# The hand-over between two mixture-of-experts layers: last token tile in two column halves, one joined sending of two tiles, two weight pieces split earlier, loads and PSUM banks in another order

## The chip, the cores and the metric

One core of one Trainium2 chip runs the whole program in one launch. The metric is the device time of that launch in microseconds (us); lower is better. Three runs of the kernel before give 742.63, 743.99 and 744.5 us, with a median of 743.99.

## What is computed

Three layers follow each other on N = 1536 tokens (2 batches of 768) of width 512. Everything is float32.

```
x   = attention with per-head decay (8 heads of 64, blocks of 64)      # [1536, 512]
x   = sum over 4 experts e of p[:, e] * (relu(x @ w1[e]) @ w2[e])      # dense: every token, hidden width 1024
l   = x @ w_gate; expert = argmax(l); gate = softmax(l)[expert]        # 8 experts, one per token
out = gate * (relu(x @ w1b[expert]) @ w2b[expert])                     # sparse: only the chosen expert
```

The change lies where the second line ends and the fourth begins.

## The kernel before

**Tiles and precision.** A token tile is 128 tokens; there are `NC` = 12. `acc[:, t, 0:512]` holds the rows of token tile t in SBUF, column `DM` = 512 its gate weight, column 513 its token number. For precision a float32 operand is split in a high and a low part: ScalarE casts the high part (`A.copy`, L195), VectorE subtracts it for the low part (L197). A matrix product is then three products: high with high, low with high, high with low (`mm3`, L572). Weights come from HBM in pieces of 512 KB (`load_piece`, L145) into tiles `raw`, each of which holds two column blocks; `split_to` (L289) does the next splits of a fixed list, and each piece whose second block is split frees its `raw` tile and issues the next load (`drop_raw`, L168). There are four such tiles, and two more (`raw2`) from the sparse layer on.

**Order of the work.** Every engine executes its own queue in program order; the order is written by hand (`tc.manual_schedule`), and a place in it is where a function is called. SP's queue issues the loads, and a load whose tile isn't free, or whose rows aren't written, holds back all that stand behind it.

**End of the dense layer** (loop at L1260 to L1287). For the last two tiles, y = 10 and z = 11, TensorE computes the hidden tiles `ht` and then for each token tile the product `y` (24 matmuls of 512 columns, `moe1_mm2`, L608), which VectorE scales and adds into `acc` (L623).

**Routing of a token tile.** `route_x` (L819) transposes `acc` on TensorE and copies it to SBUF. `route_choose` (L827) multiplies it with the gate weights (`lg`, L835) and finds the largest logit on VectorE (`mx`, `sc`, `m2`, `oh`, `df`, `seen`). `route_place` (L869) counts with two small matmuls (`rank`) how many tokens before it chose the same expert, and VectorE makes from it the row `pos` of the DRAM table `bins` to which the token goes. `route_row` (L896) writes the gate weight into `acc`, and GpSimd scatters the 128 rows into `bins` (L121).

**First expert without the round trip.** The sparse layer begins with expert 0, at most 176 tokens. Its rows of the first ten tiles are read back from `bins` (`first_load`, tile `xe`) and transposed into PSUM (`first_T`, tiles `px`, four of them, one for each 128 columns). The rows of tiles y and z never leave the chip: `first_sel` (L938) builds a 0/1 matrix `sel` from `pos`, and `first_place` (L945) adds `acc` times `sel` to `px` (8 matmuls a tile). `rows_split` (L1315) splits the four `px` into `xg`, the input of expert 0. Idle spots of TensorE are filled with products of ones (`keep_up`, L1012).

**Sparse layer** (L1531 on). `route_order` (L954) sorts the other seven experts by their token counts, on VectorE, and leaves their numbers in `nth`. SP reads these with a register load (`values_load`), loads the rows of an expert from `bins` (`load_rows`, L1331, tile `xb`) and the weights of experts 1 to 7, whose addresses depend on `nth` too. For an expert e, TensorE makes eight products `g` (L1374, L1375), VectorE and ScalarE turn them into hidden tiles and, between these, split the second weights `w1h`, `w1l` (`hook1`); then follow four products `z`, and behind each of them (`hook2`) the transposes `xt` of the next expert's rows `xb` (`rows_T`, L1347) and splits of the next first weights. In the profile the first `z` of expert 0 needs all eight hidden tiles. For experts with 129 to 255 tokens (`WIDE`) a product takes two columns blocks at once, and ScalarE (L1377) and VectorE (L1378) add the two halves in a tile of the tag `yt`.

Of the kernel before, what the change touches and what calls it, by code (L numbers as in the profile page):

```python
# [67 lines left out]
FAR = 1 << 20  # L68
OMAX = (N - min(CAPS[0], BY_RANK[0]) + P - 1) // P
# [4 lines left out]
def body(ctx: ExitStack, tc: tile.TileContext, lam, att, dp, w1a, w2a, wg, wgt, w1b, w2b, out):  # L74
# [91 lines left out]
    st = {}  # L166

# [11 lines left out]
    def split_plain(n, c, only=""):  # L179
# [7 lines left out]
        hi, lo = wt[b]  # L187
        t = raw_q[0][:, c % 2]
        if b[0] == 0 and k < K1 and half(k) == 0:
            hi, lo = (x[:, :, c * P:c * P + P] for x in (hi, lo))  # L190
            t = t.rearrange("p (d f) -> p d f", d=KD)
        else:
            hi, lo = hi[:, c, :], lo[:, c, :]
# [434 lines left out]

    def open_fast():
# [124 lines left out]
    def open_routing():  # L754
# [13 lines left out]
        rp = rt["rs"] = rt_ctx.enter_context(pool("rs", 2, side="right"))  # L768
# [50 lines left out]
    def route_x(t):  # L819
        tr = rt["ps_rt"].tile([P, KD, P], F32, tag="rtr", name=f"rtr{t}")  # L820
        for d in range(KD):
            T.transpose(tr[:, d, :], acc[:, t, d * P:d * P + P], ident)
        xt = rt["rp"].tile([P, KD, P], F32, tag="xt", name=f"xt{t}")
        A.copy(out=xt, in_=tr)
        rt[t, "xt"] = xt

    def route_choose(t, midway=None):  # L827
        rp = rt["rs"]
        if t < VT:
            lg = lg_v[:, t, :]  # L830
        else:
            xt = rt.pop((t, "xt"))
            lg = small(f"lg{t}")[:, :E2]
            for d in range(KD):
                T.matmul(lg, xt[:, d, :], wg_sb[:, d, :], start=d == 0, stop=d == KD - 1)  # L835
# [13 lines left out]
        if midway:  # L849
            midway()  # L850
        V.tensor_scalar(
            out=ec, in0=m2, scalar1=-float(MOST), scalar2=float(E2 * MOST), op0=ALU.mult,
            op1=ALU.add,
        )
# [13 lines left out]

    def route_place(t):  # L869
        rp = rt["rs"]  # L870
        oh, ec, df, prev = rt.pop((t, "chosen"))
# [3 lines left out]
        rank = small(f"rank{t}")[:, :E2]  # L875
        T.matmul(rank, upper, oh, start=True, stop=prev is None)
        if prev is not None:
            T.matmul(rank, ones, prev, start=False, stop=True)
# [26 lines left out]

    def first_load():
# [8 lines left out]
    def first_T(s):  # L915
        if s == 0:
            rt["px"] = [
                ps_mm.tile([P, 512], F32, tag="mm", name=f"px{d}") if d < 3 else
                rt["ps_rt"].tile([P, 512], F32, tag="rtr", name=f"px{d}") for d in range(KD)
            ]  # L920
        for d in range(KD):
            T.matmul(
                rt["px"][d][:, s * ST:s * ST + ST], rt["xe"][:ST, s, d * P:d * P + P],
                ident[:ST, :ST], start=s == 0, stop=False, is_transpose=True,
            )

    def first_high(t):
        ah = rt["fp"].tile([P, DM], F32R, tag="ah", name=f"ah{t}")
        A.copy(out=ah, in_=acc[:, t, 0:DM])
        rt[t, "ah"] = ah  # L930

    def first_low(t):
        ah = rt.pop((t, "ah"))
        al = rt["fp"].tile([P, DM], F32R, tag="al", name=f"al{t}")
        V.tensor_tensor(out=al, in0=acc[:, t, 0:DM], in1=ah.bitcast(F32), op=ALU.subtract)
        rt[t, "parts"] = (ah, al)

    def first_sel(t):  # L938
        sel = rt[t, "sel"] = rt["fp"].tile([P, CAP], F32R, tag="sel", name=f"sel{t}")
        V.tensor_scalar(  # L940
            out=sel, in0=rt["slots"].rearrange("p s i -> p (s i)"), scalar1=rt[t, "pos"],
            scalar2=None, op0=ALU.is_equal,
        )

    def first_place(t):  # L945
        for d in range(KD):
            for i, part in enumerate(rt[t, "parts"]):
                T.matmul(
                    rt["px"][d][:, :CAP], part[:, d * P:d * P + P], rt[t, "sel"], start=False,
                    stop=t == NC - 1 and i == 1,  # L950
# [3 lines left out]
    def route_order():  # L954
        count, place, places = od["count"], od["place"], od["places"]
        by_pair = od["tmp"][:, :EN * EN].rearrange("p (a b) -> p a b", a=EN)
        sm = small("counts")[:, :E2]
# [54 lines left out]
    def keep_up(n):  # L1012
        warmup(small("warm_rt"), n)


    with tc.manual_schedule():
# [240 lines left out]
        st_ctx.close()  # L1257
        open_last()

        for t0 in range(TS, N, 256):  # L1260
# [16 lines left out]
            for j in range(256 // P):  # L1277
                if t0 // P + j == NC - 1:
                    assert not plan
                    first_load()  # L1280
                    first_high(NC - 2)
                    split_to(0, K1 + 1, 2)
                    first_low(NC - 2)
                    moe1_mm2(KL, hs, t0, j, lambda: route_x(NC - 2))
                    continue
                moe1_mm2(KL, hs, t0, j)
                unit(2 * FC + j)  # L1287
# [12 lines left out]
        first_sel(z)  # L1300
        keep_up(4)
        first_place(z)
        route_row(y)
        route_row(z)
# [15 lines left out]
        for d in range(KD):  # L1320
            rows_split(xg[0][0][:, d, :], xg[0][1][:, d, :], rt["px"][d][:, :CAP])
# [9 lines left out]
        def load_rows(e):  # L1331
            if e >= E2:
                return
            if e:
# [4 lines left out]
                )  # L1339
            xb = gp.tile([P, NMOST, W], F32, tag="xb", name=f"xb{e}", bufs=4)  # L1340
# [27 lines left out]
        def product(e, ps, parts):  # L1368
# [7 lines left out]
            s = gp.tile([P, MOST], F32, tag="yt", name=f"s{ps.name}", bufs=4)[:, :n]  # L1376
# [374 lines left out]
```

## Time and profile before

| | before |
|---|---|
| median of 3 runs | 743.99 us |
| lowest and highest | 742.63, 744.5 us |
| profiled execution | 742.62 us |
| its span, first to last instruction | 740.8 us |
| TensorE (PE) busy | 729.9 us, 99% of the span |
| VectorE (DVE) busy | 510.6 us, 69% |
| ScalarE (ACT) busy | 312.2 us, 42% |
| share of the last-ending chain on PE | 95% |
| mean granted clock of TensorE | 0.997 |

The profile is of one execution; times in it count from the first instruction. A row of the timeline gives the start, the duration, the engine, the line of the source, the operation, its output and inputs (without buffer numbers) and how many instructions it merges; in brackets stands the idle time of the engine before it and what ended that. Instructions of one engine overlap a little, so the distance from one start to the next tells what one costs in a row, and the duration when its result is there. PEld is TensorE's loading of weights, which overlaps its matmuls.

### The profile page before, as it was taken

Reading aid. Unit: us, or ns where it says so; the run is one execution under the profiler, and the core shown is the slowest. Engines: PE = TensorE matmul, PEld = TensorE weight load, DVE = VectorE, ACT = ScalarE, POOL = GpSimd, SP = SyncE. Lnnn points to the kernel's source line nnn. Section 1 sums busy time; section 2 is a strip of 40 time slices with the busy share of each in tenths; the row PEclk is TensorE's granted clock in tenths of the full one; section 3 lists DMA queues with packets and bytes.
Section 4 is the critical chain, followed back from the end, with each engine's and each line's share of the span. In section 5 each row is a group of like instructions: output and inputs, shape, how many; then the busy total and the mean of one; then the engine's idle time right before and its main releaser. Section 6 shows DMA issues by size and latency. Waiting matters only on the chain.

```text
span 740.8 us, 12994 instructions
## 1 busy us (share of the span) xinstructions
PE 729.9 (99%) x4956; PEld 660.7 (89%) x4956; DVE 510.6 (69%) x1142; ACT 312.2 (42%) x688; POOL 80.5 (11%) x86
## 2 busy tenths in 40 slices
PE   9999999999999999999999999999999999999995
PEld 8888989889898998989889898998899998998994
DVE  7557867676766766657666667774678867675883
ACT  4333735344352434434223041631134747566672
POOL 3464000000000000000000002100021013121013
PEclk9999999999999999999999999999999999999998
DMA  8862893636446175546161443351143968765661
GB/s 314 302 217 87 282 290 111 256 115 254 162 151 256 71 270 227 176 181 231 48 247 60 196 180 135 97 201 40 52 116 124 322 212 274 249 212 184 235 222 31
DMA packets 39420, 136.79 MB, mean 185 GB/s; under 512 B 6913, under 2 KB 6913, under 8 KB 34747
## 3 DMA queue, kind: packets, MB, share of 16 engines
q1 hardware_dynamic: 37243, 129.63, 50.2%
q0 software_dynamic: 2112, 6.31, 2.2%
q8 instruction: 40, 0.66, 0.4%
q14 instruction: 25, 0.20, 0.1%
HBM read 102.85 MB, written 33.26 MB: 184 GB/s over the span
## 4 chain that ended last, share of the span: by engine, by line
PE 95%; DVE 3%; issue 1%; ACT 0%; POOL 0%; POOLq 0%; ACTq 0%
PE y L582 37%; PE b L706 26%; PE h L582 7%; PE g L582 5%; PE z L582 3%; PE z L1374 2%; PE zr L1482 2%; PE gr L582 2%; PE qk L382 1%; PE z L1375 1%; PE xo L516 1%; DVE w1l L197 1%; PE g L1374 1%; PE zr L1453 1%; PE warm L1010 1%; PE xt L1356 1%
## 5 line engine op out<-in xcount | busy, mean ns | idle before, releaser
L623 DVE SCALAR_TENSOR_TENSOR acc<-y,p_sb,acc 128x512 f32<-128x512 f32 x78 | 58.6, 751 | 67.6 <-PE y L582 60.6
L197 DVE TENSOR_TENSOR w1l<-raw,w1h 128x512 fp32r<-128x512 f32 x128 | 85.0, 687 | 29.2 <-ACT w1h L195 28.7
L713 ACT COPY u<-b 128x384 f32<-128x384 f32 x78 | 36.4, 477 | 110.1 <-PE b L706 109.1
L195 ACT CAST w1h<-raw 128x512 fp32r<-128x512 f32 x128 | 75.4, 617 | 1.7 <-DMA raw<-in_w2a 1.7
L121 POOL DMA_INDIRECT bins<-acc,pos x12 | 13.1, 1092 | 474.7 <-DVE mx L842 380.4
L706 PE MATMUL b<-xh,w0h 128*128 128x384 f32 x208 | 57.8, 338 | 0.0
L197 DVE TENSOR_TENSOR w0l<-raw,w0h 128x512 fp32r<-128x512 f32 x76 | 50.3, 707 | 0.2
L812 DVE CUSTOM_DVE_ANT_0 x<-acc,x 128x512 f32<-128x512 f32 x72 | 49.4, 687 | 1.0
L195 ACT CAST w0h<-raw 128x512 fp32r<-128x512 f32 x76 | 43.0, 622 | 2.7 <-DMA raw<-in_w1a 2.7
L720 DVE TENSOR_TENSOR u<-b,u 128x384 f32<-128x384 f32 x78 | 43.0, 552 | 1.4 <-PE b L706 1.4
L121 POOL DMA_INDIRECT out<-y,xb x16 | 29.2, 1828 | 135.4 <-DVE y L1516 84.9
L706 PEld LDWEIGHTS b<-xh,w0h 128*128 128x128 f32 x208 | 38.2, 188 | 0.6
L582 PE MATMUL g<-xg,w0h 128*128 128x288 f32 (+1 forms) x192 | 38.1, 293 | 0.0
L582 PE MATMUL h<-xh,w0h 128*128 128x256 f32 x144 | 36.0, 292 | 0.3 <-ACT xh L176 0.3
L706 PE MATMUL b<-xl,w0h 128*128 128x384 f32 x104 | 35.3, 339 | 0.0
L582 PE MATMUL h<-xh,w0l 128*128 128x256 f32 x144 | 34.6, 281 | 0.1
L706 PE MATMUL b<-t1h,w0h 128*128 128x384 f32 x104 | 31.0, 339 | 0.0
L582 PEld LDWEIGHTS g<-xg,w0h 128*128 128x128 f32 x192 | 30.9, 189 | 0.0
L1374 PE MATMUL z<-g,w1h 128*128 128x352 f32 (+2 forms) x96 | 29.1, 366 | 0.8 <-DVE g L1396 0.7
L706 PE MATMUL b<-t2h,w0l 128*128 128x384 f32 x104 | 28.9, 339 | 0.0
L706 PE MATMUL b<-t4h,w0l 128*128 128x384 f32 x104 | 28.9, 339 | 0.0
L706 PE MATMUL b<-t3h,w0h 128*128 128x384 f32 x104 | 28.8, 338 | 0.0
(328 smaller groups left out, 2038.9 us busy)
## 6 DMA issues: line engine op xcount, KB each, us to landing
raw<-in_w2a SPq DMA_DIRECT2D x32, 512.0 KB, 3.6
raw<-in_w1b SPq DMA_DIRECT2D x32, 512.0 KB, 5.5
raw<-in_w2b SPq DMA_DIRECT2D x32, 512.0 KB, 5.1
kept<-w0h SPq DMA_DIRECT2D x12, 1024.0 KB, 7.4
w0h<-kept SPq DMA_DIRECT2D x12, 1024.0 KB, 7.2
raw<-in_w1a SPq DMA_DIRECT2D x18, 512.0 KB, 6.1
att<-in_att SPq DMA_DIRECT2D x12, 512.0 KB, 5.2
kept<-w0l SPq DMA_DIRECT2D x6, 1024.0 KB, 6.8
```

Source lines behind the costliest of these rows:

```text
L121: i = G.indirect_dma_start(out=dst, out_offset=bass.IndirectOffsetOnAxis(ap=idx, axis=0), in_=src, in_offset=None, bounds_check=rows - 1, ...
L195: A.copy(out=hi, in_=t)
L197: V.tensor_tensor(out=lo, in0=t, in1=hi.bitcast(F32), op=ALU.subtract)
L382: T.matmul(qk[r][:, h, :], kT[64 * r:64 * r + 64, h, :], qT[64 * r:64 * r + 64, h, :], start=True, stop=True,)
L582: T.matmul(ps, l, r, start=first and i == 0, stop=last and i == len(ops) - 1)
L623: V.scalar_tensor_tensor(out=acc[:, t, 0:DM], in0=ps, scalar=p_sb[:, t, e:e + 1], in1=acc[:, t, 0:DM], op0=ALU.mult, op1=ALU.add,)
L706: T.matmul(ps, l[:, d, c], r[:, d, :], start=first and i == 0, stop=i == len(ops) - 1, skip_group_check=not first,)
L713: A.copy(out=t, in_=bank[2, s])
L720: V.tensor_tensor(out=t, in0=bank[b, s], in1=t, op=ALU.add)
L812: V.tensor_tensor_reduce(out=x2.rearrange("p d t -> p (d t)")[:, RING * DM:], in0=acc[:, t, 0:DM], in1=logit_piece(e), scale=1.0, scalar=0 ...
L1374: T.matmul(ps[:, :2 * n], wh, both, start=i == 0, stop=False)
L1482: T.matmul(ps[s][:st], l[:, c], r, start=h == 0 and j == 0, stop=h == 1 and j == len(ops) - 1)
```

## The change

1. **Column halves.** The product of tile z is made in two halves of 256 columns (`last_dense`), with 48 matmuls of 256 columns for 24 of 512, and `acc` is updated after each half. Between the four quarters of it stand now the transposes and logits of y and the first half of those of z. The logit product repeats the gate weights 12 times (`TIMES`), so that it has 96 columns for 8, and the `keep_up` products fall from 30 to 6.
2. **Joined sending.** `first_sel` uses `rank` and a mask directly and no longer waits for `pos`. Everything that makes `pos`, the gate weights and the scatters of y and z moves into one function, `last_sends`, behind the splits of `px`.
3. **Banks.** The four `px` share two PSUM tiles, two in each.
4. **Early splits.** All four splits of the second half of expert 0's first weights come ahead of the product of y, and the first two column blocks of its second weights (`we`) are split there too, into two tiles of the new pool `gt`, instead of between the products `g`.
5. **Loads.** Two pieces are loaded ahead of `xe`; and at the start of the sparse layer three weight pieces are now loaded ahead of the rows of experts 0 and 1. The tag `yt` has 3 buffers for 4.

```diff
+        if b == (1, K1) and c < EARLY:
+            early[c] = tuple(
+                st["gt"].tile([P, HF], F32R, tag="gt" + x, name=f"we{x}{c}")
+                for x in "hl"
+            )
...
+    def last_dense(hs, t0, j, m, i):
+        t = t0 // P + j
+        c = slice(m * HD, m * HD + HD)
+        if i == 0:
+            rt["yz"] = ps_mm.tile([P, 512], F32, tag="mm", name=f"yz{m}")[:, :HD]
+        ps = rt["yz"]
+        mm3(ps, last_parts(hs, j, c, i), i == 0, i == 1)
+        if i == 1:
+            e = half(KL) // 2
+            V.scalar_tensor_tensor(
+                out=acc[:, t, c], in0=ps, scalar=p_sb[:, t, e:e + 1], in1=acc[:, t, c],
+                op0=ALU.mult, op1=ALU.add,
+            )
...
+    def last_sends():
...
+        for i in range(n):
+            t = NC - n + i
+            oh, _, df, _ = rt.pop((t, "chosen"))
+            ex = rp.tile([P, E2], F32, tag="ex", name=f"ex{t}")
+            A.activation(out=ex, in_=df, func=AF.Exp, accum_out=sums[:, i:i + 1])
+            jk = rp.tile([P, E2], F32, tag="jk", name=f"jk{t}")
+            V.tensor_tensor_reduce(
+                out=jk, in0=rt.pop((t, "rank")), in1=oh, scale=1.0, scalar=0.0, op0=ALU.mult,
+                op1=ALU.add, accum_out=rk_all[:, t:t + 1],
+            )
...
+        V.reciprocal(acc[:, two, DM], sums)
+        for i in range(n):
+            t = NC - n + i
+            scatter(bins, pos[:, i:i + 1], acc[:, t, :], E2 * MOST, "bins")
...
         if s == 0:
-            rt["px"] = [
-                ps_mm.tile([P, 512], F32, tag="mm", name=f"px{d}") if d < 3 else
-                rt["ps_rt"].tile([P, 512], F32, tag="rtr", name=f"px{d}") for d in range(KD)
-            ]
+            px = [ps_mm.tile([P, 512], F32, tag="mm", name=f"px{d}") for d in range(2)]
+            rt["px"] = [px[d % 2][:, d // 2 * CAP:d // 2 * CAP + CAP] for d in range(KD)]
...
+            if last:
+                split_to(0, K1 + 1, 4)
+                state["owed"] = 0
+                split_to(1, K1, EARLY)
+                first_load()
...
+        first_parts(y)
+        last_dense(hs, t0, 1, 0, 0)
+        route_x(y)
+        last_dense(hs, t0, 1, 0, 1)
+        last_dense(hs, t0, 1, 1, 0)
+        first_parts(z, slice(0, HD))
+        route_x(z, low)
+        route_lg(y)
         route_choose(y)
-        keep_up(8)
-        first_high(z)
-        route_x(z)
-        first_low(z)
-        keep_up(8)
+        last_dense(hs, t0, 1, 1, 1)
+        route_lg(z, low)
+        route_rank(y)
+        first_sel(y)
+        route_x(z, high)
         first_T(0)
-        route_place(y)
-        route_choose(z, lambda: (first_T(1), keep_up(10), first_sel(y)))
-        route_place(z)
+        first_T(1)
+        route_lg(z, high)
+        first_parts(z, slice(HD, DM), "h")
+        route_choose(z)
         first_place(y)
+        route_rank(z)
         first_sel(z)
-        keep_up(4)
+        first_parts(z, slice(HD, DM), "l")
+        keep_up(6)
         first_place(z)
-        route_row(y)
-        route_row(z)
...
-            rows_split(xg[0][0][:, d, :], xg[0][1][:, d, :], rt["px"][d][:, :CAP])
+            rows_split(xg[0][0][:, d, :], xg[0][1][:, d, :], rt["px"][d])
+        last_sends()
         route_order()
...
-        load_rows(0)
-        load_rows(1)
+        load_nth(1)
+        for _ in range(state.pop("owed")):
+            load_piece()
         raws[:] = [raw2] * 2 + [rawp] * 4
         load_piece()
         load_piece()
+        load_rows(0)
+        load_rows(1)
```

**How VectorE's queue changes** between the split of `px` and the first product `g` of expert 0. Before (the rows from L899 to L901 are `route_row`, the last row is the first of `route_order`):

```order
L940 TENSOR_SCALAR sel_6022<-slots,pf_6010 128x176
L899 CAST pos_6037<-pf_5963 128x1
L900 TENSOR_SCALAR gs_5956<-gs_5956 128x1
L901 RECIPROCAL acc<-gs_5956 128x1
L899 CAST pos_6044<-pf_6010 128x1
L900 TENSOR_SCALAR gs_6003<-gs_6003 128x1
L901 RECIPROCAL acc<-gs_6003 128x1
L1317 TENSOR_TENSOR xg_6056<-px_5947,xg_6056 128x176
L1317 TENSOR_TENSOR xg_6056<-px_5948,xg_6056 128x176
L1317 TENSOR_TENSOR xg_6056<-px_5949,xg_6056 128x176
L1317 TENSOR_TENSOR xg_6056<-px_5950,xg_6056 128x176
L961 COPY count<-counts 128x8
```

And now, from the last of the four splits on (L968 to L983 are `last_sends`):

```order
L1413 TENSOR_TENSOR xg_6040<-px_5980,xg_6040 128x176
L968 ISA jk_6055,rk_all<-rank_5968,oh_5944 128x8
L968 ISA rk_all 128x1
L968 ISA jk_6059,rk_all<-rank_6012,oh_5996 128x8
L968 ISA rk_all 128x1
L972 TENSOR_SCALAR two_6051<-m_all 128x2
L976 TENSOR_SCALAR two_6050<-rk_all 128x2
L980 TENSOR_TENSOR two_6051<-two_6051,two_6050 128x2
L981 TENSOR_TENSOR twopos<-two_6051,rk_all 128x2
L982 TENSOR_SCALAR two_6049<-two_6049 128x2
L983 RECIPROCAL acc<-two_6049 128x2
L1046 COPY count<-warm_rt 128x8
```

The six row instructions stood ahead of the splits of `px`; ten now stand between them and `route_order`.

**How SP's queue changes** at the start of the sparse layer (`raw` is a weight piece, the first `xb` holds the rows of expert 0, the second those of expert 1). Before:

```order
L163 DMA raw_5863<-in_w2b 128x1024
L1343 DMA xb_6098<-bins 88x1028
L1336 TENSOR_LOAD nth
L1336 ISA x2
L1343 ISA
L1343 DMA xb_6110<-bins 96x1542
L163 ISA
L163 DMA raw_6112<-in_w1b 128x1024
L163 ISA
L163 DMA raw_6114<-in_w1b 128x1024
```

Now:

```order
L1431 TENSOR_LOAD nth
L1431 ISA x2
L166 ISA
L166 DMA raw_6114<-in_w1b 128x1024
L166 ISA
L166 DMA raw_6116<-in_w1b 128x1024
L166 ISA
L166 DMA raw_6118<-in_w1b 128x1024
L1443 DMA xb_6120<-bins 88x1028
L1443 ISA
L1443 DMA xb_6122<-bins 96x1542
```

The rows of experts 0 and 1 go behind three weight pieces of 512 KB, and the one register load of `nth` stands ahead of all.

## Rows read from the trace of the kernel before

**Rows 1.** Busy time by stretch: length, PE, PEld, DVE, ACT, POOL, clock, DMA share, GB/s.

```profile
573.00:575.00 2.00, 2.00 (x17) 2.00 (x16) 2.00 (x7) 1.96 (x7) 0.00 (x0) 1.00 0.74 192
580.00:700.00 120.00, 120.00 (x846) 114.86 (x846) 85.09 (x170) 74.30 (x161) 19.17 (x11) 1.00 0.71 240
582.00:583.00 1.00, 1.00 (x10) 1.00 (x10) 1.00 (x2) 0.32 (x2) 0.00 (x0) 1.00 1.04 414
732.00:733.00 1.00, 0.62 (x6) 0.42 (x4) 0.34 (x1) 0.00 (x0) 0.00 (x0) 1.00 0.06 16
735.00:736.00 1.00, 0.00 (x0) 0.00 (x0) 0.00 (x0) 0.00 (x0) 0.00 (x0) 0.84 0.55 205
```

**Rows 2.** Timeline of TensorE, last dense tile to expert 1's first transpose.

```profile
554.99 0.40 PE L582 MATMUL y<-w1h,ht_0h 128*128 128x512 f32 x1
...
561.04 0.95 PE L835 MATMUL lg<-wg_sb,xt 128*128 128x8 f32 x8
...
567.01 0.33 PE L948 MATMUL px<-sel,ah 128*128 128x176 f32 x1
...
567.85 0.27 PE L948 MATMUL px<-sel,al 128*128 128x176 f32 x1
...
568.28 0.43 PE L1374 MATMUL g<-xg,w0h 128*128 128x352 f32 x1
...
580.14 0.50 PE L1356 MATMUL xt<-ident,xb 96*128 96x96 f32 x4
```

**Rows 3.** Timeline of VectorE over the hand-over.

```profile
555.19 0.75 DVE L623 SCALAR_TENSOR_TENSOR acc<-y,p_sb,acc 128x512 f32<-128x512 f32 x1 [3.83 <-PE y L582]
...
564.67 0.17 DVE L842 TENSOR_REDUCE mx<-lg 128x1 f32<-128x8 f32 x1 [0.32 <-PE lg L835]
...
565.96 0.16 DVE L883 CUSTOM_DVE_ANT_0 jk<-rank,oh 128x8 f32<-128x8 f32 x1
...
566.60 0.31 DVE L940 TENSOR_SCALAR sel<-slots,pf 128x176 fp32r<-128x176 f32 x1
566.83 0.15 DVE L899 CAST pos<-pf 128x1 int32<-128x1 f32 x1
...
567.38 0.16 DVE L901 RECIPROCAL acc<-gs 128x1 f32<-128x1 f32 x1
567.88 1.08 DVE L1317 TENSOR_TENSOR xg<-px,xg 128x176 fp32r<-128x176 f32 x4 [0.34 <-ACT xg L1316]
568.88 0.15 DVE L961 COPY count<-counts 128x8 f32<-128x8 f32 x1
...
570.57 0.34 DVE L1378 TENSOR_TENSOR sg<-g,sg 128x176 f32<-128x176 f32 x1
570.83 1.28 DVE L197 TENSOR_TENSOR w1l<-raw,w1h 128x512 fp32r<-128x512 f32 x2
...
579.40 0.34 DVE L1396 SCALAR_TENSOR_TENSOR g<-sg,g 128x176 fp32r<-128x176 f32 x1 [0.16 <-ACT g L1395]
```

**Rows 4.** Timeline of weight loads, last hidden tile of expert 0.

```profile
579.79 0.19 PEld L1374 LDWEIGHTS z<-g,w1h 128*128 128x128 f32 x1 [0.20 <-DVE g L1396]
```

**Rows 5.** Chain that ended last, dense layer's end: start, length in us, what.

```profile
536.27 1.43 PE h L582 x12
...
557.96 0.44 PE rtr L822 x4
```

**Rows 6.** Timeline of ScalarE, the casts of expert 0's input.

```profile
567.54 0.93 ACT L1316 CAST xg<-px 128x176 fp32r<-128x176 f32 x4 [1.18 <-PE px L948]
```

**Rows 7.** Timeline of GpSimd, the scatters of tiles y and z.

```profile
567.51 0.97 POOL L121 DMA_INDIRECT bins<-acc,pos  x1 [15.64 <-DVE gs L900]
568.78 0.97 POOL L121 DMA_INDIRECT bins<-acc,pos  x1 [0.30 <-DVE xg L1317]
```

**Rows 8.** Timeline of SP, the row loads of experts 0 and 1.

```profile
572.16 1.85 SPq L1343 DMA_DIRECT2D xb<-bins  x2
```

**Rows 9.** DMA issues, 572.9 to 574.2: KB each, us to landing (expert 1's rows).

```profile
xb<-bins SPq DMA_DIRECT2D x1, 578.2 KB, 5.1
```

More of the change, by code (lines that the diff above doesn't have):

```diff
@@ L166, in body @@
     st = {}
+    early = {}
     def drop_raw():
@@ L831, in route_choose @@
         else:
[L832 to L835, printed above, removed]
+            if (t, "lg") not in rt:
+                route_lg(t)
+            lg = rt.pop((t, "lg"))[:, 0, :]
         mx = rp.tile([P, 1], F32, tag="mx", name=f"mx{t}")
@@ L867, in route_send, with route_rank @@
         route_row(t)
+    def route_rank(t):
+        oh, _, _, prev = rt[t, "chosen"]
+        rank = rt[t, "rank"] = small(f"rank{t}")[:, :E2]
+        T.matmul(rank, upper, oh, start=True, stop=prev is None)
+        if prev is not None:
+            T.matmul(rank, ones, prev, start=False, stop=True)
     def route_place(t):
         rp = rt["rs"]
+        if (t, "rank") not in rt:
+            route_rank(t)
+        rank = rt.pop((t, "rank"))
         oh, ec, df, prev = rt.pop((t, "chosen"))
@@ L923, in first_T, with first_parts @@
                 rt["px"][d][:, s * ST:s * ST + ST], rt["xe"][:ST, s, d * P:d * P + P],
-                ident[:ST, :ST], start=s == 0, stop=False, is_transpose=True,
-            )
[L927 to L936, printed above, removed]
+                ident[:ST, :ST], start=s == 0 and d < 2, stop=False, is_transpose=True,
+                skip_group_check=True,
+            )
+    def first_parts(t, cols=slice(0, DM), only=""):
+        if (t, "parts") not in rt:
+            rt[t, "parts"] = tuple(
+                rt["fp"].tile([P, DM], F32R, tag="a" + x, name=f"a{x}{t}") for x in "hl"
+            )
+        hi, lo = (x[:, cols] for x in rt[t, "parts"])
+        if only != "l":
+            A.copy(out=hi, in_=acc[:, t, cols])
+        if only != "h":
+            V.tensor_tensor(out=lo, in0=acc[:, t, cols], in1=hi.bitcast(F32), op=ALU.subtract)
     def first_sel(t):
         sel = rt[t, "sel"] = rt["fp"].tile([P, CAP], F32R, tag="sel", name=f"sel{t}")
+        mine = rt["fp"].tile([P, 1], F32, tag="mine", name=f"mine{t}")
         V.tensor_scalar(
-            out=sel, in0=rt["slots"].rearrange("p s i -> p (s i)"), scalar1=rt[t, "pos"],
-            scalar2=None, op0=ALU.is_equal,
+            out=mine, in0=m2_all[:, t:t + 1], scalar1=float(E2), scalar2=None, op0=ALU.is_equal
+        )
+        V.tensor_scalar(
+            out=sel, in0=rt["slots"].rearrange("p s i -> p (s i)"),
+            scalar1=rt[t, "rank"][:, 0:1], scalar2=mine, op0=ALU.is_equal, op1=ALU.mult,
         )
@@ L948, in first_place @@
                 T.matmul(
-                    rt["px"][d][:, :CAP], part[:, d * P:d * P + P], rt[t, "sel"], start=False,
-                    stop=t == NC - 1 and i == 1,
+                    rt["px"][d], part[:, d * P:d * P + P], rt[t, "sel"], start=False,
+                    stop=t == NC - 1 and i == 1, skip_group_check=True,
                 )
@@ L956, in route_order @@
         by_pair = od["tmp"][:, :EN * EN].rearrange("p (a b) -> p a b", a=EN)
-        sm = small("counts")[:, :E2]
+        sm = rt["warm"][:, :E2]
         T.matmul(sm, ones, rt["seen"], start=True, stop=True)
@@ L1329, in body, with load_nth @@
         xb_t = {}
[L1331 to L1334, printed above, removed]
+        def load_nth(e):
+            if e not in nth:
                 i = TURNS[e - 1]
@@ L1500, in moe2_mm2 @@
             for f, h in enumerate(hs):
-                wh, wl = wt[1, K1 + 2 * e + f // FC]
-                parts.append(((wh[:, f % FC, c], wl[:, f % FC, c]), h))
+                if e == 0 and f in early:
+                    w = tuple(x[:, c] for x in early[f])
+                else:
+                    w = tuple(x[:, f % FC, c] for x in wt[1, K1 + 2 * e + f // FC])
+                parts.append((w, h))
             s = product(e, ps, parts)
```

107 lines of the change are left out of this document (72 added, 35 removed).

## The prediction, made before the changed kernel was timed

> **What bounds the kernel now.** I began with the shares: TensorE is busy for 99% of the span and carries 95% of the chain that ended last, so the change counts only by what it does to TensorE's position at some fixed point of the program. From 580 to 700 us TensorE is busy for all 120 us, at full clock [rows 1]. Just at the start of that stretch, at 580.14, stands the first transpose `xt` of expert 1's rows [rows 2]; it is my fixed point, since what is won or lost by then stays. I then read the chain and the timelines engine by engine around the hand-over. Two stretches lead up to `xt`. In the first, from 561.04 us (end of the last dense product) to 568.28 (first `g`) [rows 2], a chain of small steps over three engines decides. In the second, from 567.88 on, VectorE decides: it hardly pauses from the splits of `px` to the last low part of expert 0's hidden tiles at 579.40 [rows 3], and TensorE waits for it, the last time for that low part, at 579.79 [rows 4]. So a gain in the first stretch is worth only as much as VectorE passes on.
>
> **The change, first stretch.** A product of 256 columns costs 1.43/12 = 0.119 us [rows 5]. One of 512 costs (561.04 - 554.99 - 0.44)/24 = 0.234, where 0.44 is the four transposes in between [rows 2, 5]. 48 of the first for 24 of the second is +0.11 us. Four quarters of 1.43 from 554.99, with the transposes of y (0.44), two transposes of z (0.22) and the eight logit records of y (some 0.8 of the 0.95 [rows 2], since records overlap) between them, end at 554.99 + 5.72 + 0.44 + 0.22 + 0.8 = 562.2. For the 96 logit columns I take no extra: eight records take 0.1 each, and a transpose of 128 columns costs 0.44/4 = 0.11, so the bounds are 0 and about 0.1 in all. The update of `acc`, two more transposes, the copy and the last four logit records take some 2.3 us: the same chain ran from 561.04 to `mx` at 564.67, 3.6 us, with whole tiles for halves. Tile z's `mx` so starts at 564.5 for 564.67 [rows 3]: 0.2 us won. From there the joined sending helps: `sel` of z no longer waits for the steps from `jk` (565.96) to `sel` (566.60) [rows 3], 0.64 us, nor for small ones before them. I put it at 565.7, and `first_place` of z at 566.1 for 567.01 [rows 2]: 0.9 us won.
>
> Then the banks. With four `px` the first cast starts 0.53 us after the first product of z (567.01 to 567.54 [rows 2, 6]). With two parts in a bank it must follow the third part, four products of 0.12 later (567.01 to 567.85 is seven steps [rows 2]): 566.1 + 0.53 + 0.48 = 567.1. In the new queues the third and fourth casts wait for VectorE's reads of the first and second part. The first low part so starts at 567.4 for 567.88, but the last at 568.4 for 568.63 (567.88 and three quarters of a us); half of the win is gone. The first `g` starts at 567.8 for 568.28. The PSUM page of the Trainium skill (PSUM: Partial Sum Buffer, "PSUM bank collisions raise a hardware error") states that no two engines may access one bank together, reads against reads included. That rule speaks against this part of the change; no run here shows it.
>
> **Second stretch.** Between the last split and `route_order` VectorE now makes ten small instructions. Before, six took 566.83 to 567.54, 0.12 each [rows 3], while VectorE waited anyhow; that cover is gone. Ten at 0.12 are 1.2 us, so `count` starts at 568.64 + 1.2 = 569.8 for 568.88, and the first `sg` at 571.5 for 570.57 (1.69 us after `count`, as before) [rows 3]. Against this, two splits `w1l` leave the stretch: 1.28 us [rows 3], 1.2 from start to start. The last low part starts at 579.40 + 0.93 - 1.2 = 579.1. **Worth at `xt`: -0.3 us** (579.85 for 580.14). The early splits cost nothing where they now stand: VectorE idled for 3.83 us before 555.19 [rows 3], their cover; without it 1.3 us would come on top. Three `yt` buffers cost at most 0.1 us, since a copy waits for a low part two steps older.
>
> **The loads.** This is the term that I think decides. `xt` needs the rows of expert 1 in SBUF. Before, the last scatter started at 568.78 [rows 7], SP issued the rows of expert 0 at 572.16, 3.4 us later, and those of expert 1 at the end of that row's 1.85 us, at about 573.7 [rows 8]; they landed 5.1 us later [rows 9], at 578.8, 1.3 us ahead of need. Now the reciprocal, for which the scatters wait, ends at 569.9 for 567.54. The scatters start 0.3 later and 1.27 apart as before [rows 7]: 570.2 and 571.4. The rows are issued 3.4 us after the second: 574.8 and, since `nth` is read already, 575.4. And 1.57 MB of weights stand ahead: `nth` is ready at 571.5, the register load takes 1.1 us (572.16 to 573.7 less one issue), so the three go out from 572.7 and move some 0.85 later, from 573.55 (as the first row load did).
> The bounds: if the weights ahead don't matter, the rows land at 575.4 + 5.1 = 580.5. If the weights move at 414 GB/s [rows 1] they end at 577.35, and the 0.95 MB of both experts' rows need 4.7 us more at the rate of 573 to 575 (0.385 MB in two us [rows 1]), and 0.5 to land: 582.5. Weights at half that speed add 3.8, to 586.3, which I hold for unlikely, as rows would then share the engines. I take 581.6, near the middle of the first two, since part of the slow rate in that row is the gap between the two issues. TensorE then stands for 1.7 us at `xt`, and passes it at 581.6 for 580.14: **+1.5 us**.
> The DMA page of the Trainium skill (DMA: Bandwidth & Descriptors, "How many engines (k)") states that a transfer goes over the largest number of engines up to 16 that divides the partitions. By this rule, an estimate: expert 0's 88 partitions go over 11 engines, the busiest of them have 98 + 33 + 37 KB, 6.5 us at a sixteenth of 414 GB/s from 573.55, so 580.6 with the landing and +0.4 for the sum, the lower edge of the forecast. The trace disagrees for the old order: 33 + 37 KB would have taken 2.7 us there, and landing took 5.1.
>
> **The sum.** The profiled execution took 742.62 us. Forecast: 742.62 + 1.5 = 744.1. The median of the runs shown is 1.37 above that execution, so the time predicted is 743.99 + 1.5, or **745.4 us**: no change that can be told, as about 0.3%, 2.2 us, is what a measurement here distinguishes.
>
> **Rivals.**
> *The rows land in time* (before 579.9): for it speaks that DMA engines have room early (192 GB/s in 573 to 575, where 414 is reached later [rows 1]); against it, that the rows go out 1.7 us later with three pieces ahead. Time: 743.99 - 0.3 = 743.7.
> *The rows land later than 582.4*, and the kernel is measurably slower. The place is TensorE's wait at `xt`, the price 582.4 to 584 less 580.14, so +2.3 to +3.9; it decides from weights that move below some 400 GB/s. TensorE would idle for up to 4 us there. After its last product, between 732 and 733, the granted clock was below full between 735 and 736 (0.84 [rows 1]), some 3 us on, so at the upper end a fall could add 1 or 2. Time: 747.2.
> *The clock falls without the 24 `keep_up` products.* It is 1.00 in all stretches shown up to 733 [rows 1], and I count no new gap above 0.8 us before `xt`: unlikely. At half clock some 3 us of products would take 6: 747.
> The Trainium skill (TensorE: Matmul & The Clock Gate, "A second HAM failure mode: psum-queue depth-cycling") warns that frequent short idling between groups of matmuls makes the clock swing too; by that page this rival would be likelier than I make it, and the trace shows no fall at the small gaps that it has.
> *VectorE isn't the bound of the second stretch.* If its small instructions hide, the earlier first `g` (0.45) and the waits of TensorE before `xt` (some 0.9) are won: 743.99 - 1.35 = 742.6.
>
> **How the numbers follow.** Forecast, a wait of 0.4 to 2.5 us at `xt`: 0.45. Rows in time: 0.23. Rows later than 582.4: 0.21. Clock: 0.03. VectorE not the bound: 0.05. Something that I don't see, faster by over 2.2 us: 0.03. Within 0.3% lie the first, the second and the fifth, 0.73, less a little for the edge of the forecast: 0.71. Slower: 0.21 + 0.03 and a little of that edge, 0.25. Faster: 0.04. The range reaches from 743.0 (rows in time, and the half us by which a median of three may lie lower) to 747.4 (well into the late rows); the forecast's own is 744.1 to 746.5.
>
> **What the profile after would show.** Right: in SP's timeline the two row loads behind three weight loads, at 574.5 to 575.5; TensorE idle before `xt` for 1 to 2.5 us, with the DMA as releaser; the first `g` 0.3 to 0.6 us earlier; the first `sg` some 0.9 later; ten small instructions on VectorE between; and all later stretches as long as before. Wrong: `xt` before 580 without a wait; a late `xe`, which TensorE still needs at 563.2 and which stands behind two pieces more; a granted clock under 1.00 between 560 and 590; or a last low part of expert 0 that isn't near 579.1.

## The result, and the profile after

The changed kernel takes 748.76 us (median of 6 runs, 747.96 to 749.97) against 743.98 for the kernel before (6 runs, 742.63 to 744.5). The ratio is 1.0077, with a 95% interval of 1.0067 to 1.0087: slower by 4.8 us, more than a measurement can mistake for nothing, and above the range of the prediction.

| | before | after |
|---|---|---|
| median of 6 runs | 743.98 us | 748.76 us |
| profiled execution, its span | 742.62, 740.8 us | 749.23, 747.4 us |
| mean granted clock of TensorE | 0.997 | 0.992 |

The two profiled executions lie 6.6 us apart, since that of before was 1.4 us under its median and that of after 0.5 over. The balance below is made against these 6.6 us.

TensorE's timeline after, around the start of the sparse layer (start, duration, what; in brackets the idle time ahead and what ended it):

```profile
565.94 0.43 PE L1474 MATMUL g<-xg,w0h 128*128 128x352 f32 x1 [0.58 <-DVE xg L1413]
...
577.59 0.43 PE L1474 MATMUL z<-g,w1h 128*128 128x352 f32 x1
...
584.70 0.90 PE L1456 MATMUL xt<-ident,xb 96*128 96x96 f32 x4 [6.60 <-DMA xb<-bins]
...
587.41 0.56 PE L1474 MATMUL z<-g,w1h 128*128 128x352 f32 x1
...
587.92 0.56 PE L1474 MATMUL z<-g,w1h 128*128 128x352 f32 x1
...
589.65 0.49 PE L1456 MATMUL xt<-ident,xb 96*128 96x96 f32 x4
```

TensorE stands for 6.60 us at `xt`, and what it waits for is expert 1's rows. After it, a pair of `z` products takes 0.51 us (587.41 and the next at 587.92) instead of the 0.27 of before. The stretches show why, in the columns of clock and of GB/s (the last and the third last):

```profile
571.00:573.00 2.00, 2.00 (x16) 2.00 (x16) 2.00 (x7) 1.58 (x5) 0.00 (x0) 1.00 0.71 191
573.00:575.00 2.00, 2.00 (x16) 1.88 (x14) 2.00 (x6) 1.51 (x5) 0.00 (x0) 1.00 0.97 186
575.00:577.00 2.00, 1.74 (x14) 1.66 (x12) 2.00 (x8) 1.56 (x6) 0.00 (x0) 1.00 0.94 371
577.00:579.00 2.00, 1.10 (x6) 0.59 (x4) 0.71 (x3) 0.47 (x2) 0.00 (x0) 1.00 1.07 341
579.00:581.00 2.00, 0.00 (x0) 0.00 (x0) 0.00 (x0) 0.00 (x0) 0.00 (x0) 1.00 1.03 227
581.00:583.00 2.00, 0.00 (x0) 0.00 (x0) 0.00 (x0) 0.00 (x0) 0.00 (x0) 0.89 1.01 224
583.00:585.00 2.00, 0.30 (x2) 0.30 (x3) 0.00 (x0) 0.00 (x0) 0.00 (x0) 0.50 1.03 319
...
587.00:589.00 2.00, 2.00 (x10) 2.00 (x10) 0.96 (x2) 0.15 (x1) 0.00 (x0) 0.50 0.25 94
589.00:591.00 2.00, 2.00 (x17) 2.00 (x17) 0.98 (x3) 1.13 (x3) 0.00 (x0) 0.90 0.71 260
```

The granted clock was still 1.00 in 579 to 581, where TensorE stood idle, fell in the next stretch (0.89) to 0.50, that is from 2.4 to 1.2 GHz, and came back only behind 589. The DMA engines are busy all the while from 573 to 585 (share 0.94 to 1.07). What they moved from 571 to 573 is for the most part not weights. By queue it is (packets, MB, share of the 16 engines):

```profile
q1 hardware_dynamic: 29, 0.12, 36.0%
q0 software_dynamic: 80, 0.26, 34.6%
```

The second is GpSimd's queue, with the scatters of tiles y and z; the first is SP's, with the weight pieces.

SP's timeline, the landing in the chain that ended last (start, length, what), and VectorE's timeline:

```profile
571.03 1.65 SPq L166 DMA_DIRECT2D raw<-in_w1b  x3
572.80 2.28 SPq L1443 DMA_DIRECT2D xb<-bins  x3
```

```profile
573.35 11.31 DMA xb<-bins
```

```profile
548.88 0.42 DVE L602 SCALAR_TENSOR_TENSOR ht_3l<-h,ht_3h 128x256 fp32r<-128x256 f32 x1
...
551.62 1.28 DVE L209 TENSOR_TENSOR wel<-raw,weh 128x512 fp32r<-128x512 f32 x2
...
562.52 0.17 DVE L885 TENSOR_REDUCE mx<-lg 128x1 f32<-128x8 f32 x1 [1.10 <-PE lg L865]
...
563.78 0.38 DVE L1025 TENSOR_SCALAR sel<-slots,rank,mine 128x176 fp32r<-128x176 f32 x1
...
565.55 1.30 DVE L1413 TENSOR_TENSOR xg<-px,xg 128x176 fp32r<-128x176 f32 x4 [1.06 <-ACT xg L1412]
...
567.81 0.15 DVE L1046 COPY count<-warm_rt 128x8 f32<-128x8 f32 x1
...
569.57 0.33 DVE L1478 TENSOR_TENSOR sg<-g,sg 128x176 f32<-128x176 f32 x1
...
577.20 0.34 DVE L1496 SCALAR_TENSOR_TENSOR g<-sg,g 128x176 fp32r<-128x176 f32 x1 [0.17 <-ACT g L1495]
```

Expert 1's rows landed 11.3 us after they were issued, against 5.1 before [rows 9]. The first row of VectorE tells something else: the last dense hidden tile, ahead of all that the change was thought to touch, came at 548.88. Before, the same row was

```profile
550.94 0.42 DVE L590 SCALAR_TENSOR_TENSOR ht_3l<-h,ht_3h 128x256 fp32r<-128x256 f32 x1
```

so the changed kernel enters the hand-over 2.06 us ahead. Below, "+2.06" turns a time of after into the time base of before. The balance up to the second `xt` (at 589.65):

- ahead of the hand-over: -2.06 us;
- hand-over itself: TensorE could have passed `xt` 0.36 us behind the start of its last `z` at 577.59, as in E6 below, where the rows were in time (577.23 and 577.59), so at 577.95; +2.06 is 580.01 for 580.14 [rows 2]: -0.13 us;
- wait for the rows: 584.70 less 577.95, +6.75 us;
- clock: from `xt` to the next `xt` 4.95 us, in E6 2.73: +2.2 us.

The sum is +6.8, and 6.6 is the difference of the spans.

### The profile page after: what moved, and what is told of

Read it like the earlier page. It is cut to its first block, busy times and chain, and to the rows that moved or that the text cites. A ratio compares the mean times of both kernels' runs of the same rounds, so it can differ in the third digit from the quotient of the medians.

```text
span 747.4 us, 12991 instructions
## 1 busy us (share of the span) xinstructions
PE 729.6 (98%) x4956; PEld 660.8 (88%) x4956; DVE 509.5 (68%) x1140; ACT 312.9 (42%) x690; POOL 81.7 (11%) x86
## 4 chain that ended last, share of the span: by engine, by line
PE 94%; DVE 2%; DMA 2%; issue 1%; ACT 0%; SPq 0%; POOL 0%; POOLq 0%; DVEq 0%; ACTq 0%
PE y L594 36%; PE b L739 26%; PE h L594 7%; PE g L594 5%; PE z L594 3%; PE z L1474 2%; PE zr L1583 2%; DMA xb<-bins 2%; PE gr L594 2%; PE qk L394 1%; PE z L1475 1%; PE xo L528 1%; PE g L1474 1%; PE zr L1554 1%; PE yz L594 1%; PE xt L1456 1%
## 5 line engine op out<-in xcount | busy, mean ns | idle before, releaser
L124 POOL DMA_INDIRECT bins<-acc,pos x10 | 11.2, 1118 | 456.8 <-DVE mx L885 378.5
L739 PE MATMUL b<-xh,w0l 128*128 128x384 f32 x104 | 28.8, 338 | 0.0
```

Of the source, the lines that this page charges most:

```text
L124: i = G.indirect_dma_start(out=dst, out_offset=bass.IndirectOffsetOnAxis(ap=idx, axis=0), in_=src, in_offset=None, bounds_check=rows - 1, ...
L739: T.matmul(ps, l[:, d, c], r[:, d, :], start=first and i == 0, stop=i == len(ops) - 1, skip_group_check=not first,)
```

## The experiments

Theory Q: expert 1's rows queue behind the weight pieces issued ahead of them and share the engines with what is issued behind. Rival S: they are late because the scatters are. E1 to E4 ran on one chip beside the same runs of the kernel before (743.26 us).

**E1. Rows ahead of the pieces.**

```diff
         load_nth(1)
+        load_rows(0)
+        load_rows(1)
         for _ in range(state.pop("owed")):
             load_piece()
...
-        load_rows(0)
-        load_rows(1)
```

> The changed kernel with the two row loads put ahead of the three weight pieces again; all else of the change stays. Theory Q (expert 1's rows land late because they queue behind 1.57 MB of weights, and share the engines with what is issued right behind them): the rows are issued at about 573 us as before, land 5 to 6 us later, at 578 to 579.5, and TensorE waits 0 to 1.3 us at xt instead of 6.6; without a long wait the clock stays at 1.00, which gives back some 2.3 us more. Time 748.8 - 6 - 2.3 = 740.5 us (739.5 to 742). Rival S (the rows are late because the joined sending puts the scatters later, the weights matter little): the wait stays above 4 us, time above 745 us.

742.04 us, ratio 0.9983 (0.9974 to 0.9993), at the upper end of the forecast. TensorE's timeline has

```profile
580.52 0.55 PE L1456 MATMUL xt<-ident,xb 96*128 96x96 f32 x4 [0.94 <-DMA xb<-bins]
```

and the clock is 1.00 in every stretch from 571 to 593. The wait is all but gone, though every step of the joined sending is as in the changed kernel; rival S falls. The rows landed 5.9 us after their issue at 574.59.

**E2. One piece ahead instead of three.**

```diff
         load_nth(1)
         for _ in range(state.pop("owed")):
             load_piece()
+        load_rows(0)
+        load_rows(1)
         raws[:] = [raw2] * 2 + [rawp] * 4
         load_piece()
         load_piece()
-        load_rows(0)
-        load_rows(1)
```

> The changed kernel with one weight piece (512 KB) ahead of the two row loads instead of three. Theory Q: the landing moves with the bytes ahead; two pieces fewer are worth 1.05 MB at 190 to 370 GB/s, some 3 to 5 us, so the wait at xt is 2 to 3.5 us, the clock falls a little or not at all, time 742 to 745 us. Rival S: wait above 5 us, time above 747 us.

747.04 us, ratio 1.0052 (1.0035 to 1.0068).

```profile
581.24 0.90 PE L1456 MATMUL xt<-ident,xb 96*128 96x96 f32 x4 [2.57 <-DMA xb<-bins]
```

The wait is as theory Q had it: 0.94, 2.57 and 6.60 us with none, one and three pieces ahead. The time is above the forecast, since I had thought that a wait of this length would hardly touch the clock. It did:

```profile
579.00:581.00 2.00, 0.00 (x0) 0.00 (x0) 0.34 (x1) 0.07 (x1) 0.00 (x0) 0.84 0.98 261
581.00:583.00 2.00, 1.76 (x9) 1.76 (x9) 0.31 (x1) 0.82 (x2) 0.00 (x0) 0.50 1.01 398
```

**E3. The kernel before with two pieces ahead of the rows.**

```diff
-            if e:
+            if e not in nth:
...
-        load_rows(0)
-        load_rows(1)
+        nth[1] = nc.values_load(
...
         raws[:] = [raw2] * 2 + [rawp] * 4
         load_piece()
         load_piece()
+        load_rows(0)
+        load_rows(1)
```

> The kernel before with only its load order changed: nth is read and two weight pieces are issued ahead of the two row loads; nothing else of the change. Theory Q: the pieces move from about 572.5 to 576.5 us, the 0.93 MB of rows need 4.3 us or more behind them, so they land at 581 to 583.5 and TensorE waits 1 to 3.5 us at xt where it waited 0; with a fall of the clock at the upper end, time 745.5 to 749 us. Rival S: no wait, 744 us.

749.54 us, ratio 1.0076 (1.0057 to 1.0096), a little above the forecast.

```profile
584.60 0.90 PE L1356 MATMUL xt<-ident,xb 96*128 96x96 f32 x4 [3.43 <-DMA xb<-bins]
```

The order of the loads alone, without any other part of the change, makes the kernel before as slow as the changed one. The clock fell here too (0.57 in 583 to 585, then 0.50). The profiled execution had also lost 0.9 us ahead of the hand-over (`ht_3l` at 551.81 for 550.94), so the load order is worth some 6.2 of its 7.1 us.

**E4. Fillers in the wait**, to part the wait from the clock.

```diff
+            if e == 1 and s == 0:
+                for _ in range(100):
+                    T.matmul(tr[:, 0, :], ones, ones, start=True, stop=True)
...
```

> The changed kernel with 100 products of 128 columns on ones (0.058 us each, some 5.8 us; their result is overwritten) ahead of the first transpose xt, where TensorE waits for the rows. Theory: the rows still land at about 584.7 us, TensorE still passes xt then, but the clock stays at 1.00 since the engine is busy, so the products behind the wait take 0.27 us a pair instead of 0.51: 748.8 - 2.3 = 746.5 us (745.7 to 747.3). Rival: the clock falls for another reason than the wait (the fillers don't hold it, or it fell because the 24 keep_up products are gone): 748.8 us.

746.9 us, ratio 1.0049 (1.0032 to 1.0066): the time of the theory. But the profiled execution is the one of four that took 749.45 (the others 746.81 to 746.93): there TensorE still waited 1.76 us behind the fillers, and the clock was 0.80, 0.50 and 0.85 in the three stretches from 585 to 591. So 100 fillers were too few to decide it; E8 has more.

E5 to E8 ran beside 743.13 us of before.

**E5. The kernel before with 128 unused bytes**, for the 2 us ahead of the hand-over.

```diff
         rt["none"] = rp.tile([P, W - DM], F32, name="none", bufs=1)
+        rt["pad"] = rp.tile([P, 32], F32, name="pad", bufs=1)
+        G.memset(rt["pad"], 0.0)
```

> The kernel before with one unused tile of 128 bytes per partition added to the pool rs, nothing else. In the changed kernel this pool holds four more small tiles (two0 to two2 and twopos, 128 bytes in all), and the pools opened after it, the tiles t1h to t4l among them, lie 128 bytes lower. Theory L (place): the products of 384 columns that read t1h to t4l run at another pace there; they made the changed kernel 1.9 us earlier between 80 and 440 us, in every one of its profiles, and the same gain shows here: 743.3 - 1.9 = 741.4 us (741 to 742), with a mean of 336 ns for 338 to 340 in the rows of these products. Rival: something else in the changed program gave the 1.9 us; then 743.3 us and 340 ns.

741.35 us, ratio 0.9978 (0.9967 to 0.999), as theory L had it. The products of 384 columns that read `t2h`, with the first and the last start in us behind the durations (ns); first the kernel before, then after, then E5:

```profile
L706 PE MATMUL b<-t2h,w0l x104: 337/337/444, 80.5 to 463.6; 128*128 128x384 f32 x104
```

```profile
L739 PE MATMUL b<-t2h,w0l x104: 336/336/440, 80.4 to 461.6; 128*128 128x384 f32 x104
```

```profile
L706 PE MATMUL b<-t2h,w0l x104: 336/336/442, 80.1 to 461.3; 128*128 128x384 f32 x104
```

From first to last it is 383.1 us before, 381.2 after and 381.2 in E5. The 1.9 us are in no edit that I had read as one: they come from four small tiles in the pool `rs`, which put `t1h` to `t4l` 128 bytes lower, as the unused tile does in E5. Between the first and the last of these products lie others too; the last section parts them.

**E6. E1 with expert 1's rows ahead of expert 0's.**

```diff
         load_nth(1)
-        load_rows(0)
         load_rows(1)
+        load_rows(0)
```

> The changed kernel with both row loads ahead of the three weight pieces, expert 1's rows ahead of expert 0's. Theory Q: the 0.94 us that TensorE still waited at xt with the rows first come from expert 0's 353 KB ahead of expert 1's; behind nothing, expert 1's rows land 1 to 2 us earlier, about 579 us, and TensorE doesn't wait for them: 742.0 - 0.9 = 741.1 us (740.6 to 741.6). Rival: the two row loads share the engines whatever their order, the wait stays 0.5 to 1 us, time 741.6 to 742.2 us.

740.17 us, ratio 0.9961 (0.9945 to 0.9977), below the forecast. TensorE no longer waits:

```profile
565.59 0.43 PE L1474 MATMUL g<-xg,w0h 128*128 128x352 f32 x1 [0.58 <-DVE xg L1413]
...
577.23 0.43 PE L1474 MATMUL z<-g,w1h 128*128 128x352 f32 x1
...
577.59 0.50 PE L1456 MATMUL xt<-ident,xb 96*128 96x96 f32 x4
...
580.32 0.50 PE L1456 MATMUL xt<-ident,xb 96*128 96x96 f32 x4
```

**E7. Expert 2's rows later.** The load that stood right behind expert 1's rows is issued in the hook behind the second `z` of expert 0.

```diff
-            load_rows(e + 2)
+            if e:
+                load_rows(e + 2)
...
+                if e == 0 and i == 1:
+                    load_rows(2)
```

> The changed kernel (three weight pieces ahead of the rows) with the load of expert 2's rows (257 KB), which stood right behind expert 1's, issued only after expert 1's rows were used. Theory Q2: rows that land last share the engines with what is issued behind them; without the 257 KB the wait at xt falls from 6.6 by 0.6 to 1.4 us, time 747.4 to 748.2 us. Rival: only what is ahead counts; wait 6.4 to 6.8 us, time 748.8 us.

```profile
584.76 0.90 PE L1456 MATMUL xt<-ident,xb 96*128 96x96 f32 x4 [5.79 <-DMA xb<-bins]
```

The wait is shorter by 0.81 us, and the landing 10.5 for 11.3 us after its issue, as theory Q2 had it. The time is not: 749.78 us, ratio 1.0085 (1.0065 to 1.0104), above the forecast and not to be told from the changed kernel's. In the profiled execution the hand-over began 0.88 us later than in after's (`ht_3l` at 549.76), and the slow products behind the wait cost 0.4 us more, which hides the 0.81; of what a shorter wait is worth in the end this run says nothing.

**E8. 130 fillers.**

```diff
-                for _ in range(100):
+                for _ in range(130):
```

> The changed kernel with 130 filler products (7.5 us) for 100, so that no idle time is left before xt. With 100 the clock still fell in the profiled run, after the 1.8 us that they left open. If it fell for those, it stays at 1.00 now, and TensorE passes xt up to 0.9 us later than it could: 746 to 747 us, with less spread than with 100. If fillers of this kind don't hold the clock, it falls behind them as before, at 748 to 750 us.

747.59 us, ratio 1.006 (1.0041 to 1.0079), 747.37 to 747.98: 0.6 us above the forecast, with the small spread that it had.

```profile
577.89 7.43 PE L1457 MATMUL xt<-ones 128*128 128x128 bf16 x130
585.16 0.50 PE L1460 MATMUL xt<-ident,xb 96*128 96x96 f32 x4
587.90 0.50 PE L1460 MATMUL xt<-ident,xb 96*128 96x96 f32 x4
```

```profile
585.00:587.00 2.00, 2.00 (x21) 2.00 (x19) 0.80 (x2) 1.31 (x3) 0.00 (x0) 1.00 0.89 352
```

With no idle time left the clock stays at 1.00, and the next `xt` comes 2.74 us later, not 4.95. So the clock fell for the wait, and not for want of the `keep_up` products; it costs 2.2 us in the changed kernel.

E9 to E11 ran beside 742.71 us, E12 beside 743.41.

**E9. E6 with 128 unused bytes behind `acc`**, which move `xh`, `xl` and the tiles `ht`.

```diff
     accp = ctx.enter_context(pool("accp", 1))
+    pad = accp.tile([P, 32], F32, name="pad")
+    G.memset(pad, 0.0)
```

> The changed kernel with expert 1's rows first and the pieces behind the row loads, and with an unused tile of 128 bytes per partition behind acc, so that xh, xl and the tiles ht lie 128 bytes higher; they stood as t1h to t4l did before (the address leaves 160 when divided by 256), and would now leave 32. Theory L: it is the place of the moving operand that sets the pace. The 390 products of 384 columns that read xh and xl between 100 and 440 us gain 3 to 4 ns each, 1.4 us; those of 512 columns that read ht gain between nothing and as much, up to 3.4 us for about 1000: 740.2 - 1.4 = 738.8 us at most, 735.4 at least. Rival: the place matters for t1h to t4l alone (their neighbours, not the remainder): 740.2 us.

736.89 us, ratio 0.9922 (0.9908 to 0.9936): theory L again, in the middle of its range.

**E10. E5 with expert 1's rows ahead of expert 0's.**

```diff
-        load_rows(0)
         load_rows(1)
+        load_rows(0)
```

> The kernel before with the 128 unused bytes in the pool rs and expert 1's rows loaded ahead of expert 0's; nothing of the new hand-over. Before, the rows landed 1.3 us ahead of need, so the swap alone should give nothing: 741.3 us (740.9 to 741.7), and what the changed kernel with the swap is faster by (740.2 us) is what its new hand-over is worth, about 1 us. Rival: the swap alone brings as much; then 740.2 us, and the hand-over is worth nothing.

740.83 us, ratio 0.9978 (0.9968 to 0.9988), the ratio of E5: the swap alone gives nothing, as the rows were in time. To E6 it is 0.7 us by the medians, with overlapping intervals. By the traces the new hand-over is worth less: from the last dense `ht_3l` to `xt` it is 29.41 us here, 29.06 in E6, and 29.20 in the kernel before, so 0.1 to 0.4 us.

**E11. E6 without the early splits.**

```diff
-EARLY = 2
+EARLY = 0
```

> The changed kernel with expert 1's rows first and the pieces behind the row loads, but without the two early splits of the second weight (EARLY = 0). Theory: VectorE bounds the stretch from the split of px to expert 0's last hidden tile, so two splits more in it (1.2 us) make the last low part 1 to 1.3 us later, and TensorE passes xt as much later: 741.2 us (740.9 to 741.6). Rival: VectorE isn't the bound there, or the splits find room behind the last low part: 740.2 us.

742.04 us, ratio 0.9985 (0.9974 to 0.9996), 0.4 us above the range forecast. In the trace the step has the size forecast:

```profile
566.89 0.43 PE L1474 MATMUL g<-xg,w0h 128*128 128x352 f32 x1 [0.58 <-DVE xg L1413]
...
580.07 0.49 PE L1456 MATMUL xt<-ident,xb 96*128 96x96 f32 x4
```

From the first `g` to `xt` it is 13.18 us, in E6 12.00. Two splits more in the stretch cost 1.18 us; VectorE is its bound.

**E12. E9 with the moved tiles at multiples of 256 bytes.**

```diff
-    pad = accp.tile([P, 32], F32, name="pad")
+    pad = accp.tile([P, 24], F32, name="pad")
...
+        rt["pad"] = rp.tile([P, 8], F32, name="pad_rs", bufs=1)
+        G.memset(rt["pad"], 0.0)
```

> As the fastest kernel so far (expert 1's rows first, pieces behind, 128 bytes behind acc), but with 96 bytes behind acc and 32 bytes more in rs, so that xh, xl, the tiles ht and t1h to t4l all start at multiples of 256 bytes. If the pace of a product goes by how its moving operand lies to a boundary that 256 is a multiple of, this is as good or better: 735 to 737 us. If a remainder of 32 was good for another reason (the banks in which stationary and moving operand lie together), nothing is certain, and a time back towards 740 us, with 338 to 340 ns in the rows, is possible.

730.71 us, ratio 0.9848 (0.9812 to 0.9884), far more than expected and the fastest kernel of the study. Four of six runs lie between 730.6 and 730.74, one took 732.35 and one 738.34, for unknown reasons. The same products as above, in E9 and in E12:

```profile
L741 PE MATMUL b<-t2h,w0l x104: 336/336/444, 79.9 to 458.7; 128*128 128x384 f32 x104
```

```profile
L741 PE MATMUL b<-t2h,w0l x104: 333/335/440, 79.8 to 455.2; 128*128 128x384 f32 x104
```

378.8 and 375.4 us from first to last, for 383.1 before. In E12 it is no longer these products that gain but others between them (last section).

## Why the prediction was wrong

**What bounds the kernel: right.** What TensorE lost at `xt` and by the clock behind it, less what it had won ahead, is the difference of the whole program (the balance above).

**First stretch: right in kind, half in size.** In the time base of before, `mx` of z starts at 564.58 (forecast 564.5), `sel` at 565.84 (565.7), the first low part at 567.61 (567.4), the first `g` at 568.00 (567.8). Each step is 0.1 to 0.2 us late on the forecast, so 0.28 us is won at the first `g`, not 0.48. The four low parts took 1.30 us for 1.08 [rows 3], which would fit casts that wait for reads of the same bank; it wasn't tried apart.

**Second stretch: right.** `count` at 569.87 (569.8), the first `sg` at 571.63 (571.5), the last low part at 579.26 (579.1, before 579.40 [rows 3]). Worth 0.13 us at `xt` for 0.3. E11 measured the term of the two splits at 1.18 for 1.2. The early splits stand at 551.62, where VectorE had been idle [rows 3], and cost nothing there.

**The loads: the step that failed.** The prediction's late bound for expert 1's rows was 582.5, from weights at 414 GB/s that end at 577.35 and rows that need 4.7 and 0.5 us behind them, and it took 581.6. (By its own rate 0.95 MB take 4.9 us, not 4.7, which changes little.) It held 586.3 for unlikely, "as rows would then share the engines". They landed at 584.66 + 2.06 = 586.7. The 4.2 us from its bound have two parts, which the sizes of the packets in the trace tell apart (4096 bytes for weights, 4112 and 6168 for the rows of experts 0 and 1, 2056 for those of expert 2):

- *The weights came late and slowly: 3.1 us.* The packets of the three pieces run from 572.25 to 578.37, in the time base of before from 574.3 to 580.4, where the prediction had 573.55 to 577.35. That is 6.1 us for 1.57 MB, 257 GB/s. From 573 to 575 the engines moved weights alone, at 186 GB/s, and from 575 to 577 at 371. A slow stretch stood in [rows 1] (192 GB/s); I gave its rate to the rows and the best rate of the trace to the weights. Beside it stood a DMA share of 0.74, and I took the low rate for room. After, the share at 186 GB/s is 0.97: a low rate is no room where the engines are busy.
- *The rows shared the engines with what was issued behind them: 1.1 us.* From 578.4 to the landing it is 6.3 us, not 5.2. Of this, 0.95 lie between the last packet and the landing, where the prediction had 0.5. Up to 583.7, where that packet ends, the engines moved 0.80 MB of the two row loads and 0.42 MB of expert 2's rows and the next pieces, which SP issued from 574.72 on. I counted only what stood ahead. E7 took away 257 KB from behind and the wait fell by 0.81 us.

The Trainium skill (DMA: Bandwidth & Descriptors, "Queues, rings and completion order") has a sentence that I passed over: on each engine descriptors are taken in ring order, but without a barrier, so that a later one may finish its write before an earlier one. The trace agrees as far as it goes, as packets of the next pieces start at 581.6, two us before the last one of expert 1's rows ends; the order within one engine it doesn't show. The estimate by the same page's "How many engines (k)", 580.6, is off by 6 us.

**The rival had the right mechanism and too small a price.** Rows that land later than 582.4, from weights that move below some 400 GB/s, are what happened; it had 0.21. Its price ended at 584 and 1 to 2 us of clock. The wait was 6.75 us and the clock 2.2, and E2 shows the fall with a wait of 2.57 already, at a price that is no smaller (2.8 us over the next two `xt`). So 748.8 lay above a range that was meant to reach "well into the late rows".

**The clock without `keep_up`: right.** It stayed at 1.00 up to the wait, through gaps of 0.2 to 0.6 us, and E8 shows that it depends on the wait.

**A term that the prediction didn't have.** 1.9 us were won between 80 and 460 us, where the sum held everything to be as before, because `rs` grew by 128 bytes (E5). Without it the changed kernel would be slower by about 6.7 us. The error of the loads and the clock was larger than the result shows.

## What to carry to other kernels

A load that an engine will soon wait for goes into the queue ahead of loads that only fill buffers, and its landing is worked out with the slow rate that a busy stretch of the trace shows, not the best one, and with all that is issued until it lands, behind it as well as ahead. A wait of TensorE is priced with the slow products behind it, which here cost no less after 2.57 us than after 6.60. And a change of a pool's size is a change of every tile above it: compare the rows of stages that weren't touched, and try the address of the operands before finer things.

## What was not expected of the hardware

**The address of a tile changes the pace of TensorE.** In the built programs the tiles `t1h` to `t4l`, `xh`, `xl` and `ht`, operands of the dense layer, start at addresses that leave 160 when divided by 256. In the changed kernel and in E5 `t1h` to `t4l` leave 32, in E9 all do, and in E12 all leave 0. TensorE is busy for 100% of the stage throughout. The mean distance in ns from one product's start to the next of the same shape, between 80 and 540 us (gaps from missing records left out):

| products | before | after, E5, E6 | E9 | E12 |
|---|---|---|---|---|
| 384 columns, moving `t1h` to `t4l` | 176.7 | 173.5 | 173.4 | 173.6 |
| 384 columns, moving `xh`, `xl` | 176.7 | 176.5 | 173.5 | 173.5 |
| 512 columns, stationary `ht` | 234.3 | 234.3 | 233.1 | 228.9 |
| 256 columns, moving `xh`, `xl` | 119.9 | 120.0 | 118.3 | 113.8 |

A clear step stands only where the row's own tiles move. Unused bytes alone take the ratio from 0.9961 (E6) to 0.9848 (E12), 1.1% of the whole time, and E5's are another 0.2%. Shown is that the place does it. Theory L, which held the place of the moving operand for the cause, is too narrow: in the 512-column products the tile that moves is the stationary operand, while the moving weights `w1h` and `w1l` keep their addresses. For 384 columns 32 is as good as 0, for 512 and 256 it isn't. Which boundary counts is open (256 is only what was tried), and so is how the place acts, in the product itself or through what other engines read and write: in all three runs some tiles of VectorE and ScalarE moved along.

**The clock.** Waits of 1.76 (E4), 2.57, 3.43, 5.79 and 6.60 us each brought TensorE to half clock, one of 0.94 did not. From `xt` to the next but one it took 2.2 us more than the 5.46 of the kernel before after the wait of 6.60, 2.8, 2.6 and 2.6 us more after those of 2.57, 3.43 and 5.79, and 1.6 us more after that of 1.76. The products of ones kept it at full clock where they left no gap.

**DMA.** The weight pieces moved at 186 GB/s from 573 to 575 and at 371 from 575 to 577, with the engines busy in both (0.97 and 0.94). A packet of 4096 bytes took 0.31 to 0.40 us up to 575 and 0.16 behind it; in E3, where the pieces start at 574.2, 0.28 to 0.33 us up to 576 and 0.17 behind it. Why is open.
